# Expert weights that share memory with the rows of x, and quarters in place of whole matrices between the gathers

## The chip, the cores and the metric

The kernel runs on one core of a Trainium2 chip. The metric is device time in microseconds, the median of several executions. Before the change it is 227.68 us (three executions, 227.32 to 227.93). A profiled execution of the same kernel took 224.94 us.

## The reference

Two operations in a row. First a retention recurrence over 4 batches, 8 heads, 768 steps and head size 64; its result becomes 3072 rows x of 512 columns. Then a layer of 8 experts with an early exit: a row with a skip score above 0 goes to the expert with its largest gate logit, and that expert's result is weighted and added to the row; every other row stays as it is.

```
state = gamma * state + k[t] outer v[t];  y[t] = scale * (q[t] @ state)
x = y, heads side by side: 3072 x 512
for rows with x @ w_skip > 0:  e = argmax(x @ w_gate);  g = softmax(x @ w_gate)[e]
    x += g * (relu(x @ w1[e]) @ w2[e])      # w1: 512 x 1024, w2: 1024 x 512
```

## The kernel before, in words

The first stage works on 16 pairs of heads (`for i in range(NU)`), four to a batch. For each pair it turns scaled q and k (`rows_t`), forms chunk states (`kv_states`), scores and values, and multiplies the result by the identity and the gate's columns (`rows_x`, L337), which gives 128 columns of `xall[b]`, the 768 rows of a batch (12 KB in each partition, two buffers in turn), and the gate logits. `store_x` (L355) writes a batch's rows to `out`: for the last batch three stores of 512 KB on SP's queue (L687), for the others on ACT's. Steps of the gate (`gate_a` and on) find for each expert the places of its rows. They come in slots of 128 rows: slot 0 of an expert holds the first 128, slot 1 the next.

The second stage runs over 11 tasks: slot 0 of experts 0, 1 and 2 (k = 0 to 2), slot 1 of the same three (k = 3 to 5), and both slots of experts 3 to 7 (k = 6 to 10). A task casts the gathered rows to bf16 (`cast_rows`, L654), turns them on PE (`turn`, L666), runs `layer1` (L703) and `layer2` (L719), and `scatter` (L519) writes the result rows back. In PE's order the turn of the next task stands between layer 1 and layer 2 of this one. `gather` (L507) and `scatter` are indirect DMAs that POOL issues.

The weights lie in DRAM as f32 and are loaded as bf16, by DMAs that POOL issues too, on the same queue. One expert's w1 or w2 is four quarters (`load_piece`, L199, 256 KB each in bf16) or one whole matrix (`load_whole`, L213, 1 MB). The whole one lies with other rows to a partition, which `inner1` and `inner2` tell to `turn` and `layer1`. All 64 quarters stand in one list, in the order of experts, and whatever comes next is taken from its head. The orders are written out by hand: in the first stage `EARLY` says how many quarters a pair issues and `PLACES` at which of five places in the pair; before each, a small multiplication on POOL (`pool_after`, L538) waits for a result of that place. In the second stage `plan` (L758) gives for each task the steps that follow its layer 2: `Q` a quarter, `W` a whole matrix, `g3.1` the gather of expert 3's slot 1, `s` the scatters of all results so far.

Between the stages POOL issues the gathers of experts 1 and 2 (slot 0), then a drain (L689), a `pool_after` on the last rows, and the steps of `plan[None]`. By then 32 quarters have been issued, the weights of experts 0 to 3.

Of the kernel before, what the change touches and what calls it, by code (L numbers as in the profile page):

```python
# [9 lines left out]
FP32 = mybir.dt.float32  # L10
BF16 = mybir.dt.bfloat16
# [7 lines left out]
def kernel(  # L19
# [18 lines left out]
    PE, V_, A_, G_ = nc.tensor, nc.vector, nc.scalar, nc.gpsimd  # L38

    B, H, S, D = q.shape  # L40
    N, DM = out.shape
    E = moe_w1.shape[0]
    F = moe_w1.shape[2]
    R = 2
    NCH = S // 128
# [8 lines left out]
    NDB = DM // 128  # L54
    NFB = F // 128
# [9 lines left out]
    poolC = ctx.enter_context(tc.tile_pool(name="constp", bufs=1))  # L65
    poolG = ctx.enter_context(tc.tile_pool(name="gpool", bufs=1))
    poolW = ctx.enter_context(tc.tile_pool(name="wpool", bufs=1))

    stM = ExitStack()
    stM.enter_context(tc.manual_schedule())  # L70
# [2 lines left out]
    pool = st1.enter_context(tc.tile_pool(name="rsb", bufs=2))  # L73
# [120 lines left out]

    w1b, w2b, inner1, inner2 = {}, {}, {}, {}

    def load_piece(e, which, c, pl):  # L199
        if which == 0:  # L200
            if not c:
                w1b[e] = pl.tile([128, NDB, F], BF16, tag=f"w1_{e}", bufs=1, name="w1b")
                inner1[e] = 1
            G_.dma_start(out=w1b[e][:, c, :], in_=moe_w1[e][c * 128 : (c + 1) * 128, :])
        else:
            if not c:
                w2b[e] = pl.tile([128, NFB, DM], BF16, tag=f"w2_{e}", bufs=1, name="w2b")
                inner2[e] = NFB // 4
            cs = slice(c * NFB // 4, (c + 1) * NFB // 4)
            rows = moe_w2[e][c * F // 4 : (c + 1) * F // 4, :]  # L210
            G_.dma_start(out=w2b[e][:, cs, :], in_=rows.rearrange("(p a) d -> p a d", p=128))

    def load_whole(n, pl):  # L213
        for _ in range(n):
            if pieces:
                e, which, c = pieces[0]
                assert c == 0
                del pieces[:4]
                t = pl.tile([128, NDB * F], BF16, tag=f"w{which + 1}_{e}", bufs=1, name=("w1b", "w2b")[which])
                cols = (F, DM)[which]  # L220
                (w1b, w2b)[which][e] = t[:, :].rearrange("p (a f) -> p a f", f=cols)
                (inner1, inner2)[which][e] = (NDB, NFB)[which]
                src = (moe_w1, moe_w2)[which][e].rearrange("(p a) f -> p (a f)", p=128)
                G_.dma_start(out=t[:, :], in_=src)

    pieces = [(n // 8, n // 4 % 2, n % 4) for n in range(E * 8)]

    def load_pieces(n, pl):
        for _ in range(min(n, len(pieces))):
            load_piece(*pieces.pop(0), pl)  # L230

# [3 lines left out]
    QKT, St, ATm, Y, xT, xall, Lp = {}, {}, {}, {}, {}, {}, {}  # L235
# [4 lines left out]
    def tps(name="tps"):  # L240
        return psum.tile([128, 512], FP32, tag="T", bufs=2, name=name)
# [95 lines left out]
    def rows_x(i, a):  # L337

        if not 0 <= i < NU:
            return  # L340
        b, p = divmod(i, NP)
        if p == 0 and a == 0:
            xall[b] = pool.tile([128, NCH, DM], FP32, tag="xall", bufs=2, name="xall")
            Lp[b] = pool.tile([128, NP, NCH, NL], FP32, tag="Lp", bufs=2, name="Lp")
        ps = tps()
        for j in range((NCH // 2)):
            PE.matmul(  # L347
                out=ps[:, j * XW : (j + 1) * XW], lhsT=xT[i][:, a * (NCH // 2) + j, :], rhs=IW[:, p, :], start=True, stop=True,
                skip_group_check=True,
            )  # L350
# [149 lines left out]
    def free(ins, others):  # L500
        for o in others:
            tc.declare_no_dep(ins, o.ins, reason="the slots of a pass name distinct rows, empty ones none")

    def rows_of(st, first):
        return (out[0:NOLD, :], NOLD) if first and st == 0 else (out[:, :], N)

    def gather(e, st, first=True):  # L507
        t = xrows[len(gathers) % NROW if first else st]
        src, n = rows_of(st, first)
        ga = G_.indirect_dma_start(  # L510
            out=t[:, :], out_offset=None, in_=src,
            in_offset=bass.IndirectOffsetOnAxis(ap=slot[st][0][:, e : e + 1], axis=0), bounds_check=n - 1, oob_is_err=False,
        )
        xg[e, st] = t
        if first:
            free(ga.ins, scatters)
            gathers.append(ga)
# [13 lines left out]

    EARLY = {0: 1, 1: 1, 2: 1, 3: 2, 4: 1, 5: 1, 6: 2, 7: 2, 8: 1, 9: 1, 10: 2, 11: 3, 12: 4, 13: 5, 14: 4, 15: 1}
    PLACES = {1: (3,), 2: (0, 3), 3: (0, 2, 4), 4: (0, 1, 3, 4), 5: (0, 1, 2, 3, 4)}
    junk = poolC.tile([1, 1], FP32, name="junk")

    def pool_after(x, y=None):  # L538

        G_.tensor_tensor(junk[:, :], x, x if y is None else y, ALU.mult)  # L540

    def weights(i, place, after):

        if place in PLACES.get(EARLY.get(i, 0), ()):
            pool_after(after)
            load_pieces(1, poolW)
# [107 lines left out]
    def cast_rows(e, sts, cast, pl, bufs):  # L654
        xb = []
        for st in sts:
            t = pl.tile([128, DM], BF16, tag="xb", bufs=bufs, name="xb")
            cast(out=t[:, :], in_=xg[e, st][:, :])
            xb.append(t)
        return xb  # L660

    def blocks(rows, a):

        return rows.rearrange("p (c t a) -> p c a t", t=128, a=a)
# [14 lines left out]
    values(NU - 1)  # L679
    b = B - 1  # L680
    pool_after(xT[NU - 1][0:1, 0, 0:1])
    gather(2, 0)
    xb0 = cast_rows(0, [0], V_.tensor_copy, poolG, 1)
    rows_x(NU - 1, 0)
    xgT = turn(0, xb0, V_.tensor_copy, poolG, 1, lambda: psum.tile([128, NDB, 128], BF16, tag="AT0", bufs=1, name="xtp"))
# [10 lines left out]
    poolE = ctx.enter_context(tc.tile_pool(name="esb", bufs=2, reuse_waits="tile"))  # L696
    poolX = ctx.enter_context(tc.tile_pool(name="wlate", bufs=1, reuse_waits="tile"))
# [5 lines left out]
    def layer1(e, xgT):  # L703
        n = xgT.shape[2]
        hT = poolE.tile([128, NFB, CAP], BF16, tag="hT", bufs=2, name="hT")
        m = 512 // n
        for f2 in range(NFB // m):
            ps = psE.tile([128, m, n], FP32, tag="hps", bufs=2, name="hps")
            for f in range(m):
                fb = m * f2 + f  # L710
                for db in range(NDB):
                    PE.matmul(  # L712
                        out=ps[:, f, :], lhsT=blocks(w1b[e][:, db, :], inner2[e])[:, fb // inner2[e], fb % inner2[e], :],
                        rhs=xgT[:, db, :], start=(db == 0), stop=(db == NDB - 1),
                    )
            A_.activation(out=hT[:, m * f2 : m * f2 + m, 0:n], in_=ps[:, :, :], func=AF.Relu, bias=0.0, scale=1.0)  # L716
        return hT

    def layer2(e, sts, hT, first=True):  # L719
        yos = []  # L720
        for k, st in enumerate(sts):
            ps = psE.tile([128, DM], FP32, tag="yps", bufs=2, name="yps2")
            for fb in range(NFB):
                PE.matmul(  # L724
                    out=ps[:, :], lhsT=hT[:, fb, k * 128 : (k + 1) * 128], rhs=w2b[e][:, fb, :],
                    start=(fb == 0), stop=(fb == NFB - 1),
                )
            yo = poolE.tile([128, DM], FP32, tag="yo", bufs=8, name="yo")
            V_.scalar_tensor_tensor(  # L729
                out=yo[:, :], in0=ps[:, :], scalar=slot[st][1][:, e : e + 1], in1=xg[e, st][:, :], op0=ALU.mult, op1=ALU.add  # L730
            )
            if first:
                yos.append((e, st, yo))
            else:
                scatter(e, st, yo, first)
        return yos

    def passes():
# [17 lines left out]
    tasks += [(e, list(range(NST))) for e in range(FIRST, E)]  # L756

    plan = {  # L758
        None: "Q Q", 0: "s", 1: "g0.1 Q g1.1 Q g2.1 W g3.0 s W g3.1", 2: "s g4.0 W g4.1", 3: "s g5.0 W g5.1",
        4: "s g6.0 W g6.1", 5: "s g7.0 W g7.1", 6: "s W",  # L760
    }
    yos = []

    def give(k):
        for step in plan.get(k, "s").split():
            if step == "W":
                load_whole(1, poolX)
            elif step == "Q":
                load_pieces(1, poolX)
            elif step[0] == "g":  # L770
                gather(*(int(n) for n in step[1:].split(".")))
            else:
                while yos:
                    scatter(*yos.pop(0))
# [9 lines left out]
    for k, (e, sts) in enumerate(tasks):  # L784
        hT = layer1(e, xgT)
# [77 lines left out]
```

## Time and profile before

| | us |
|---|---|
| median of three executions | 227.68 |
| profiled execution | 224.94 |
| its span, first to last instruction | 223.2 |
| PE busy | 192.9 (86%) |
| POOL busy | 119.4 (54%) |
| DVE busy | 109.9 (49%) |
| ACT busy | 87.5 (39%) |
| POOL's DMA queue, share of 16 engines | 49.7% |
| mean granted clock of TensorE | 0.971 |

The span in 40 slices of 5.58 us:

```profile
PE   0899998999899997999999888789880799999960
DMA  6979999999999899798799993698999999996211
```

A digit is the busy share of a slice in tenths; the lines count from the span's start. The first stage fills the span up to about 143 us and the second the rest. All times below are from the span's start.

### The profile page before, as it was taken

What the parts mean: (1) busy time and instruction counts of PE and PEld (TensorE: products, weight loads), DVE (VectorE), ACT (ScalarE), POOL (GpSimd) and SP (SyncE); (2) the same over time, 40 slices, a digit from 0 to 9 for tenths busy, and PEclk for the clock granted to TensorE, in tenths of its full rate; (3) what the DMA queues carried; (4) which work ended last, traced back from release to release, by engine and by line L of the source; (5) the groups of instructions that cost most, each with busy time, mean ns of one, the idle gap of its engine ahead of it and who ended that gap; (6) DMA issues with size and microseconds to landing.
All of it is one profiled execution on the core that took longest, in us unless ns stands there. A gap on an engine that the chain in (4) does not pass through costs nothing.

```text
span 223.2 us, 8246 instructions
## 1 busy us (share of the span) xinstructions
PE 192.9 (86%) x3493; PEld 157.1 (70%) x3502; DVE 109.9 (49%) x351; ACT 87.5 (39%) x197; POOL 119.4 (54%) x185
## 2 busy tenths in 40 slices
PE   0899998999899997999999888789880799999960
PEld 0777887897798886798888777765760377678720
DVE  5444535535655566566576786384420253433220
ACT  5324544745435454436455332464240042134210
POOL 2345975765566645746887223428855556523330
PEclk9999999999999999999999999999996599999997
DMA  6979999999999899798799993698999999996211
GB/s 176 247 203 247 280 298 289 236 282 313 245 214 206 222 280 353 179 224 195 117 221 302 215 184 74 145 321 174 181 220 244 246 255 256 267 255 186 90 48 43
DMA packets 49241, 48.73 MB, mean 218 GB/s; under 512 B 3780, under 2 KB 40644, under 8 KB 48304
## 3 DMA queue, kind: packets, MB, share of 16 engines
q0 software_dynamic: 8752, 22.97, 49.7%
q1 hardware_dynamic: 39152, 20.47, 31.7%
q10 hardware_dynamic: 1296, 4.72, 5.6%
q8 instruction: 29, 0.48, 0.8%
q14 instruction: 12, 0.10, 0.1%
HBM read 56.64 MB, written 10.49 MB: 301 GB/s over the span
## 4 chain that ended last, share of the span: by engine, by line
PE 65%; issue 12%; DMA 7%; DVE 6%; POOL 4%; ACT 2%; POOLq 1%; SPq 0%; ACTq 0%; DVEq 0%
PE tps L252 12%; PE tps L347 11%; PE atps L301 10%; PE yps L325 10%; DMA xrows<-out_dram,si 6%; PE kvps L264 6%; PE yps L724 5%; PE yps L281 5%; PE hps L712 4%; POOL out_dram L521 3%; DVE ATm L307 2%; DMA kw<-in_k_dram 1%; POOL xrows L510 1%; PE xtp L673 1%; ACT xT L335 1%
## 5 line engine op out<-in xcount | busy, mean ns | idle before, releaser
L307 DVE TENSOR_TENSOR ATm<-atps,maskc 128x384 f32<-128x384 f32 x64 | 32.9, 553 | 29.6 <-PE atps L301 28.9
L253 ACT COPY QKT<-tps 128x512 f32<-128x512 f32 x48 | 28.1, 587 | 39.7 <-PE tps L252 39.0
L301 PE MATMUL atps<-QKT 64*64 64x128 f32 x768 | 35.4, 271 | 2.0 <-issue 0.9
L716 ACT ACTIVATE hT<-hps 128x512 bf16<-128x512 f32 x32 | 19.0, 597 | 46.0 <-PE hps L712 46.0
L347 PE MATMUL tps<-IW,xT 128*128 128x137 f32 x192 | 29.2, 288 | 2.5 <-ACT xT L335 1.7
L712 PEld LDWEIGHTS <-w1b 128*128 128x128 bf16 x352 | 29.0, 115 | 3.4 <-issue 1.0
L712 PE MATMUL hps<-xgT,w1b 128*128 128x128 bf16 (+1 forms) x352 | 30.7, 246 | 0.6 <-DVE xgT L674 0.6
L724 PE MATMUL yps<-w2b,hT 128*128 128x512 bf16 x119 | 30.5, 396 | 0.5
L301 PEld LDWEIGHTS atps<-QKT 64*64 64x64 f32 x768 | 27.8, 133 | 2.6 <-DVE ATm L307 1.3
L104 POOL TENSOR_TENSOR ks<-kw,tk 128x768 f32<-128x768 f32 x15 | 22.4, 1490 | 12.0 <-DMA kw<-in_k_dram 11.7
L347 PEld LDWEIGHTS tps<-IW,xT 128*128 128x128 f32 x192 | 24.5, 190 | 5.1 <-ACT xT L335 3.4
L325 PE MATMUL yps<-ATm,vn 64*64 64x128 f32 x768 | 26.6, 272 | 1.5 <-issue 1.3
L521 POOL DMA_INDIRECT out_dram<-yo,si x16 | 16.5, 1032 | 20.0 <-DVE yo L729 16.0
L335 ACT COPY xT<-yps 64x384 f32<-64x384 f32 x32 | 15.2, 474 | 25.9 <-PE yps L325 23.5
L252 PE MATMUL tps<-ident,ks 128*128 128x128 f32 x96 | 18.3, 300 | 6.8 <-DVE ks L104 5.3
L325 PEld LDWEIGHTS yps<-ATm,vn 64*64 64x64 f32 x768 | 22.0, 133 | 2.6 <-issue 1.7
L510 POOL DMA_INDIRECT xrows<-out_dram,si x16 | 16.9, 1056 | 12.8 <-DVE g L492 5.6
L104 POOL TENSOR_TENSOR qs<-qw,tq 128x768 f32<-128x768 f32 x15 | 22.4, 1493 | 2.5 <-DMA qw<-in_q_dram 1.3
L729 DVE SCALAR_TENSOR_TENSOR yo<-yps,g,xrows 128x512 f32<-128x512 f32 x16 | 12.0, 750 | 22.9 <-PE yps L724 19.9
L724 PEld LDWEIGHTS <-hT 128*128 128x128 bf16 x128 | 12.3, 101 | 13.6 <-issue 1.7
L281 PE MATMUL yps<-QKT,St 64*64 64x128 f32 x320 | 20.2, 279 | 0.0
L352 ACT COPY xall<-tps 128x384 f32<-128x384 f32 x32 | 15.3, 479 | 10.9 <-PE tps L347 9.0
(113 smaller groups left out, 225.3 us busy)
## 6 DMA issues: line engine op xcount, KB each, us to landing
vn<-in_v_dram SPq DMA_DIRECT2D x16, 384.0 KB, 6.3
kw<-in_k_dram SPq DMA_DIRECT2D x15, 384.0 KB, 5.9
qw<-in_q_dram SPq DMA_DIRECT2D x15, 384.0 KB, 5.2
w1b<-in_moe_w_dram POOLq DMA_DIRECT2D x20, 256.0 KB, 6.1
out_dram<-xall ACTq DMA_DIRECT2D x9, 512.0 KB, 6.9
w2b<-in_moe_w_dram POOLq DMA_DIRECT2D x16, 256.0 KB, 5.3
w2b<-in_moe_w_dram POOLq DMA_DIRECT2D x4, 1024.0 KB, 12.7
w1b<-in_moe_w_dram POOLq DMA_DIRECT2D x3, 1024.0 KB, 12.7
```

The source lines that it names most:

```text
L104: eng.tensor_tensor(o[:, :, h, :], rows[:, :, h, :], sc[:, :, h, :], ALU.mult)
L252: PE.transpose(out=ps[:, j * 128 : (j + 1) * 128], in_=(ks, qs)[w][i][:, s_, :, :].rearrange("p h d -> p (h d)"), identity=ident[:, :])
L253: A_.copy(out=QKT[i][:, 4 * m : 4 * m + 4, :], in_=ps[:, :].rearrange("p (j t) -> p j t", j=4))
L281: PE.matmul(out=Y[i, c][o : o + 64, g, :], lhsT=St[i][t : t + 64, ch - 1, :], rhs=QKT[i][t : t + 64, NCH + R * g : NCH + R * g + R, 64 * c ...
L301: PE.matmul(out=ps[h][cp, j, :], lhsT=QKT[i][hp, a * SPB + j, cp], rhs=QKT[i][hp, NCH + R * g : NCH + R * g + R, cp], start=True, stop=True,)
L307: V_.tensor_tensor(out=ATm[i, a][:, t, :, :], in0=ps[t][:, :, :], in1=maskc[:, a * SPB : (a + 1) * SPB, :, :].rearrange("p s r t -> p s (r ...
L325: PE.matmul(out=Y[i, c][o : o + 64, g, :], lhsT=vn[i][cp, h * G + g, r * D : (r + 1) * D], rhs=ATm[i, a][cp, h, j, :], start=False, stop=l ...
L347: PE.matmul(out=ps[:, j * XW : (j + 1) * XW], lhsT=xT[i][:, a * (NCH // 2) + j, :], rhs=IW[:, p, :], start=True, stop=True, skip_group_che ...
L510: ga = G_.indirect_dma_start(out=t[:, :], out_offset=None, in_=src, in_offset=bass.IndirectOffsetOnAxis(ap=slot[st][0][:, e : e + 1], axis ...
L521: sc = G_.indirect_dma_start(out=dst, out_offset=bass.IndirectOffsetOnAxis(ap=slot[st][0][:, e : e + 1], axis=0), in_=yo[:, :], in_offset= ...
L712: PE.matmul(out=ps[:, f, :], lhsT=blocks(w1b[e][:, db, :], inner2[e])[:, fb // inner2[e], fb % inner2[e], :], rhs=xgT[:, db, :], start=(db ...
L724: PE.matmul(out=ps[:, :], lhsT=hT[:, fb, k * 128 : (k + 1) * 128], rhs=w2b[e][:, fb, :], start=(fb == 0), stop=(fb == NFB - 1),)
```

## The change

A new pool, `rowsp`, holds the two buffers of `xall`; they had been in a pool of the first stage that was given up between the stages. A function `home` now says where each quarter lies. Quarters 0 to 31 and those from 44 on have a tile for four, as before. Quarters 32 to 37 share one buffer of `xall`, quarters 38 and 39 have a small tile, and quarters 40 to 43 share the other buffer of `xall`. The weights are kept as lists of rows, so that a matrix can lie in two places.

The order changes with it. Pair 13 issues four quarters for five, pair 15 four for one. One quarter is issued ahead of the gather of expert 2 and one behind it, before the drain. After task 0 two quarters are issued behind the scatter. After task 1 a quarter stands between gathers where two of the steps were whole matrices; after tasks 2 and 3 two quarters stand for one whole matrix. Whole matrices are loaded for experts 6 and 7 alone, after tasks 4 to 7. The result tile `yo` has seven buffers for eight.

```diff
+    QS = NDB * F // 4
+    NEARLY, NKEEP = 32, 12 * 1024 // (2 * QS)
+    homes, pieces = {}, [(n // 8, n // 4 % 2, n % 4) for n in range(E * 8)]
+
+    def home(n, pl):
+        if n < NEARLY or n >= NEARLY + 2 * 4 + 4:
+            tag, size, first = f"w{n // 4 % 2 + 1}_{n // 8}", 4, n // 4 * 4
+        elif n < NEARLY + NKEEP:
+            tag, size, first = "xall", NKEEP, NEARLY
+        elif n < NEARLY + 8:
+            tag, size, first = "wrest", NEARLY + 8 - (NEARLY + NKEEP), NEARLY + NKEEP
         else:
+            tag, size, first = "xall", NKEEP, NEARLY + 8
+        if first not in homes:
+            bufs = 2 if tag == "xall" else 1
+            homes[first] = (poolP if tag == "xall" else pl).tile([128, size, QS], BF16, tag=tag, bufs=bufs, name="wb")
+        return homes[first][:, n - first, :]
+
+    def load_pieces(k, pl):
+        for e, which, c in pieces[:k]:
+            t = home(e * 8 + which * 4 + c, pl)
+            rows = (moe_w1, moe_w2)[which][e]
+            n = rows.shape[0] // 4
+            part = rows[c * n : (c + 1) * n, :]
+            G_.dma_start(out=t, in_=part.rearrange("(p a) f -> p (a f)", p=128))
+            (inner1, inner2)[which][e] = a = n // 128
...
-            xall[b] = pool.tile([128, NCH, DM], FP32, tag="xall", bufs=2, name="xall")
+            xall[b] = poolP.tile([128, NCH, DM], FP32, tag="xall", bufs=2, name="xall")
...
-    EARLY = {0: 1, 1: 1, 2: 1, 3: 2, 4: 1, 5: 1, 6: 2, 7: 2, 8: 1, 9: 1, 10: 2, 11: 3, 12: 4, 13: 5, 14: 4, 15: 1}
+    EARLY = {0: 1, 1: 1, 2: 1, 3: 2, 4: 1, 5: 1, 6: 2, 7: 2, 8: 1, 9: 1, 10: 2, 11: 3, 12: 4, 13: 4, 14: 4, 15: 4}
...
     pool_after(xT[NU - 1][0:1, 0, 0:1])
+    load_pieces(1, poolW)
     gather(2, 0)
+    load_pieces(1, poolW)
...
-            yo = poolE.tile([128, DM], FP32, tag="yo", bufs=8, name="yo")
+            yo = poolE.tile([128, DM], FP32, tag="yo", bufs=7, name="yo")
...
-        None: "Q Q", 0: "s", 1: "g0.1 Q g1.1 Q g2.1 W g3.0 s W g3.1", 2: "s g4.0 W g4.1", 3: "s g5.0 W g5.1",
-        4: "s g6.0 W g6.1", 5: "s g7.0 W g7.1", 6: "s W",
+        None: "Q Q", 0: "s Q Q", 1: "g0.1 Q g1.1 Q g2.1 Q g3.0 s Q g3.1", 2: "s g4.0 Q g4.1 Q", 3: "s g5.0 Q g5.1 Q",
+        4: "s g6.0 W g6.1", 5: "s g7.0 W g7.1", 6: "s W", 7: "s W",
```

## Rows read from the trace of the kernel before

**Rows 1.** Windows: busy us (instructions) of each engine, granted clock, DMA share, GB/s.

```profile
136.00:138.00 2.00, 1.92 (x48) 1.65 (x48) 1.38 (x10) 0.03 (x1) 1.09 (x1) 1.00 0.00 0
...
146.00:148.00 2.00, 1.79 (x14) 0.95 (x15) 1.86 (x12) 1.38 (x3) 0.30 (x2) 1.00 1.03 414
...
175.00:180.00 5.00, 5.00 (x20) 2.35 (x19) 1.51 (x3) 0.00 (x0) 3.10 (x3) 0.54 1.01 258
```

**Rows 2.** Chain of waits: start, length, what.

```profile
161.11 12.88 DMA xrows<-out_dram,si
```

**Rows 3.** Timeline of PE: start, us, line, operation, count [idle before <- releaser].

```profile
149.84 0.39 PE L673 MATMUL xtp<-identb,xb 128*128 128x128 bf16 x4
...
153.90 1.90 PE L724 MATMUL yps<-w2b,hT 128*128 128x512 bf16 x8
155.98 0.40 PE L673 MATMUL xtp<-identb,xb 128*128 128x128 bf16 x4 [0.19 <-ACT xb L658]
...
164.44 1.95 PE L712 MATMUL hps<-xgT,w1b 128*128 128x128 bf16 x32
...
174.50 0.61 PE L673 MATMUL xtp<-identb,xb 128*128 128x128 bf16 x4 [5.30 <-DVE xb L658]
174.90 3.62 PE L724 MATMUL yps<-w2b,hT 128*128 128x512 bf16 x8
...
178.38 4.27 PE L712 MATMUL hps<-xgT,w1b 128*128 128x256 bf16 x32
...
186.39 3.69 PE L712 MATMUL hps<-xgT,w1b 128*128 128x256 bf16 x32
...
212.20 3.62 PE L724 MATMUL yps<-w2b,hT 128*128 128x512 bf16 x15
```

**Rows 4.** Timeline of ACT, the cast of expert 0's slot 1.

```profile
155.31 0.62 ACT L658 CAST xb<-xrows 128x512 bf16<-128x512 f32 x1 [0.64 <-DMA xrows<-out_dram,si]
```

**Rows 5.** Timeline of POOL between the stages: gather, junk, quarters, scatter, gather, quarter.

```profile
141.93 1.03 POOL L510 DMA_INDIRECT xrows<-out_dram,si  x1 [0.50 <-issue]
147.39 0.18 POOL L540 TENSOR_TENSOR junk<-xall 1x1 f32<-1x1 f32 x1 [4.42 <-ACT xb L658]
147.89 1.14 POOL L204 DMA_DIRECT2D w1b<-in_moe_w_dram  x2 [0.32 <-issue]
150.63 1.06 POOL L521 DMA_INDIRECT out_dram<-yo,si  x1 [1.60 <-DVE yo L729]
151.99 1.06 POOL L510 DMA_INDIRECT xrows<-out_dram,si  x1 [0.30 <-DVE Rsum L424]
153.06 0.59 POOL L204 DMA_DIRECT2D w1b<-in_moe_w_dram  x1
```

**Rows 6.** Lines 689 and 819, the drains: duration ns min/median/max, first and last start.

```profile
L689 POOLq DRAIN  x1: 5516/5516/5516, 141.7 to 141.7; - x1
...
L819 POOLq DRAIN  x1: 4387/4387/4387, 209.7 to 209.7; - x1
```

**Rows 7.** DMA issues, the two at 141.93 and 209.90: us from issue to landing last.

```profile
xrows<-out_dram,si POOLq DMA_INDIRECT x1, 3.8
...
out_dram<-yo,si POOLq DMA_INDIRECT x1, 2.5
```

**Rows 8.** DMA issues of weights, at 119.18, 125.11, 129.43, 186.47 and 192.67 in order.

```profile
w1b<-in_moe_w_dram POOLq DMA_DIRECT2D x1, 256.0 KB, 9.2
...
w1b<-in_moe_w_dram POOLq DMA_DIRECT2D x1, 256.0 KB, 7.0
...
w2b<-in_moe_w_dram POOLq DMA_DIRECT2D x1, 256.0 KB, 5.2
...
w1b<-in_moe_w_dram POOLq DMA_DIRECT2D x1, 1024.0 KB, 12.7
...
w2b<-in_moe_w_dram POOLq DMA_DIRECT2D x1, 1024.0 KB, 13.2
```

**Rows 9.** DMA issue of the gather at 151.99 (expert 0, slot 1).

```profile
xrows<-out_dram,si POOLq DMA_INDIRECT x1, 3.3
```

More of the change, by code (lines that the diff above doesn't have):

```diff
@@ L67 @@
     poolW = ctx.enter_context(tc.tile_pool(name="wpool", bufs=1))
+    poolP = ctx.enter_context(tc.tile_pool(name="rowsp", bufs=1))
     stM = ExitStack()
@@ L197 @@
     w1b, w2b, inner1, inner2 = {}, {}, {}, {}
[L199 to L204, printed above, removed]
-        else:
[L206 to L230, printed above, removed]
+    QS = NDB * F // 4
[8 more added lines that the diff above has]
+            tag, size, first = "wrest", NEARLY + 8 - (NEARLY + NKEEP), NEARLY + NKEEP
+        else:
+            tag, size, first = "xall", NKEEP, NEARLY + 8
[3 more added lines that the diff above has]
+        return homes[first][:, n - first, :]
@@ new lines, in load_pieces @@
+    def load_pieces(k, pl):
[6 more added lines that the diff above has]
+            (inner1, inner2)[which][e] = a = n // 128
+            got = t.rearrange("p (a f) -> p a f", a=a)
+            (w1b, w2b)[which].setdefault(e, []).extend(got[:, j, :] for j in range(a))
+        del pieces[:k]
@@ new lines, in load_whole @@
+    def load_whole(pl):
+        e, which, c = pieces[0]
+        assert c == 0
+        del pieces[:4]
+        rows = (moe_w1, moe_w2)[which][e]
+        (inner1, inner2)[which][e] = a = rows.shape[0] // 128
+        t = pl.tile([128, 4 * QS], BF16, tag=f"w{which + 1}_{e}", bufs=1, name="wb")
+        G_.dma_start(out=t[:, :], in_=rows.rearrange("(p a) f -> p (a f)", p=128))
+        got = t[:, :].rearrange("p (a f) -> p a f", a=a)
+        (w1b, w2b)[which][e] = [got[:, j, :] for j in range(a)]
@@ L712, in layer1 @@
                     PE.matmul(
-                        out=ps[:, f, :], lhsT=blocks(w1b[e][:, db, :], inner2[e])[:, fb // inner2[e], fb % inner2[e], :],
+                        out=ps[:, f, :], lhsT=blocks(w1b[e][db], inner2[e])[:, fb // inner2[e], fb % inner2[e], :],
                         rhs=xgT[:, db, :], start=(db == 0), stop=(db == NDB - 1),
@@ L724, in layer2 @@
                 PE.matmul(
-                    out=ps[:, :], lhsT=hT[:, fb, k * 128 : (k + 1) * 128], rhs=w2b[e][:, fb, :],
+                    out=ps[:, :], lhsT=hT[:, fb, k * 128 : (k + 1) * 128], rhs=w2b[e][fb],
                     start=(fb == 0), stop=(fb == NFB - 1),
                 )
-            yo = poolE.tile([128, DM], FP32, tag="yo", bufs=8, name="yo")
+            yo = poolE.tile([128, DM], FP32, tag="yo", bufs=7, name="yo")
             V_.scalar_tensor_tensor(
@@ L766, in give @@
             if step == "W":
-                load_whole(1, poolX)
+                load_whole(poolX)
             elif step == "Q":
```

## The prediction

> **What bounds the kernel now.** I read the 40 slices of the page first: DMA is full from slice 28 to 36, and PE has one hole there, slice 31. The windows show what follows the hole: from 175 to 180 us PE is busy all the time, at a granted clock of 0.54 [rows 1]. The chain of waits names its cause: from 161.11 us it is one DMA for 12.88 us, the second gather of expert 3 [rows 2]. The PE timeline gives the size [rows 3]. Layer 1 of task 5 (expert 2, second half) ends at 164.44 + 1.95 = 166.39. Next in PE's order stand the transposes of expert 3, and the last four run only at 174.50, because the gather was issued on the queue behind two whole matrices. Then the half clock: eight matmuls of layer 2 take 3.62 us, against 1.90 in task 2, and layer 1 of expert 3 takes 4.27 against 3.69 for expert 4 (0.58). From 166.39 to 178.38 are 12.0 us; with the 0.58 it is 12.6. Unhindered it would be two groups of transposes and eight matmuls, 0.8 + 1.9, some 2.5 us by their overlap. So the hole costs 10.1 us, and after it PE runs without a gap to the last layer 2 at 212.20: what is won there is won at the end, until something else is late.
>
> Two places have no slack. Task 3 (expert 0, second half) transposes at 155.98, right when the cast on ACT ends, and that cast waited for its gather [rows 3, 4]. And POOL, which issues gathers, scatters and weights in one order, stands in a drain from 141.7 for 5.5 us [rows 5, 6].
>
> **The change part by part.**
>
> *Homes and buffers.* Memory only; no instruction is added but twelve quarter issues for three whole ones. The home of quarters 32 to 37 is free once the third batch's rows are stored, which pair 13 begins and pair 15 finds done; the other one waits for the last stores, with k = 1 as its first use. One yo buffer less: the eighth result waits for the first scatter, some 20 us older. I take 0 for these.
>
> *Four more quarters before the second stage* (pair 13 one less, pair 15 three more, two around the gather of expert 2). A quarter takes 1.25 us of the queue: the ones issued at 125.11 and 129.43 land at 132.1 and 134.6, with one between [rows 8]. The extra 5.0 us go where DMA is partly idle: from 136 to 138 its share is 0.00 [rows 1]. But the last of them meet the stores of the last rows, which fill DMA from 146 to 148 (1.03) [rows 1]. The gather of expert 2 now has a quarter ahead of it and the stores beside it; I put its landing at 147.8 instead of 141.93 + 3.8 = 145.7 [rows 5, 7]. PE wants it at 149.84, after a cast of 0.62 [rows 3, 4]: 1.4 us of cover are left, and past them each us costs one.
>
> *The drain.* It names no semaphore. Both drains of the trace outlast the issue before them, and both end a like time after that issue has landed: the first at 147.2, 1.5 us after 145.7; the second at 209.7 + 4.4 = 214.1, 1.7 us after 209.90 + 2.5 = 212.4 [rows 5 to 7]. Counted from the end of the issue they differ more, 4.3 and 3.2. So I read it as waiting for the landing of the last POOL DMA. That is now a quarter, issued about 144.7 (junk, quarter, gather and quarter in a row, by the durations of rows 5). No row shows a drain behind a quarter, so the bounds: if only the issue counts, it ends at 145.3 + 3.2 to 4.3, about 149; if the quarter lands as slowly as the ones beside earlier stores, 9.2 us [rows 8], at 155.4. Between them: some 6.5 us of quarters, gather and stores are left at 144.5, shared between two queues, so the quarter lands at about 150.5 and the drain ends at 152.0. I take that one, 4.8 us later than now.
>
> *Four quarters and a scatter ahead of the first second-half gather.* Behind the drain come junk (0.66 to the next issue), two quarters (1.14), the scatter (0.30 + 1.06), two more quarters (1.16) and 0.30 [rows 5]. The gather is issued at 152.0 + 4.6 = 156.6, against 151.99. It lands 3.3 us later at best, as now [rows 9]. The path from that landing over ACT to PE is the one without slack: task 3 begins 4.6 us later.
>
> *The clock.* PE is then idle from 153.90 + 1.90 = 155.80 to 160.6. The hole of before lowered the clock; I count it lowered once here too, at its price of before: 1.72 in layer 2, 0.58 in layer 1 and some 0.1 in the transposes, 2.4 us. Not lowered it is 0, and I count 2.4 because the nearest row is a hole of the same kind.
>
> *Quarters between the gathers of k = 1.* Now 9.12 us pass from the issue of the first gather to that of expert 3's second. The same steps follow, so it is issued at 165.7, with quarters of 1.25 us ahead of it in place of two whole matrices. It lands some 4.5 us later (3.3 and a quarter's 1.25), at 170.2. PE asks for it at 166.39 + 4.6 + 2.4 = 173.4. The old hole is gone whole: 10.1 us off the path.
>
> *Whole matrices for the last two experts alone.* The last one moves from k = 6 to k = 7. POOL issues 16 gathers or scatters (1.33 us with their gap) and seven weights (0.9) between 165.7 and it, so it is issued at about 194.6 (now 192.67) and lands 13.2 us later at the present load, 207.8 [rows 8]. Layer 2 of the last expert, at 212.20 now, would want it at 212.2 - 3.1 = 209.1. That is cover of 1.3 us, where now it is 6.3.
>
> *By a rule of the skill.* A whole matrix issued at 186.47 and the next at 192.67 land 6.7 us apart with two gathers' and scatters' worth between; four quarters take 5.0 [rows 8]. The Trainium skill, "DMA: Bandwidth & Descriptors", section Bandwidth, says that transfers should be batched to 1 MiB or more for three quarters of the peak, and its section on the anatomy of one DMA puts a fixed part of about 2.0 us on each. By that fixed part, queued, nine further transfers would cost 18 us; by the rows, which overlap it, nothing. The trace disagrees with the queued reading.
>
> **Sum.** Off the path: 10.1. On it: 4.6 (task 3) + 2.4 (clock) = 7.0. Net 3.1 off the span of 223.2, and with what lies around it (224.94 - 223.2 = 1.74, unchanged) 221.8 for the profiled execution. The median of the runs is 227.68, 2.7 above that execution; I take the 3.1, with a little for transposes that no longer run at half clock (0.2), off the median: 224.4.
>
> **Rivals.**
> 1. *The drain waits for the issue only.* For it: a quarter is another kind of DMA than the two indirect ones that were seen; against it the 1.5 and 1.7. Drain to 149, gather at 153.6, landing behind the quarters at about 157, task 3 1.7 late, no fall of the clock: 10.1 - 1.7 = 8.4 off, held to about 8 by the last matrix (POOL 3 us earlier, landing at 204.8, wanted at 203.8). 219.6.
> 2. *The hole only moves.* The quarter lands 9.2 us after its issue, the drain ends at 155.4, task 3 is 8.0 late and the clock falls: 10.4 against 10.1. 227.8, no change.
> 3. *POOL's order becomes the bound: slower.* Everything behind the drain shifts with it, the last matrix too. It lands at 207.8 plus the shift past 152.0, and before it was wanted at 212.2. From 4.4 us of shift, that is a landing of the quarter later than 10.2 us after its issue, the end is later than now, one for one. For it: the stores fill DMA just then. Against it: no quarter of the trace takes 10 us. With 6 us of shift: 229.3.
> 4. *Quarters hold the queue longer than wholes.* At twice 1.25 us the eight quarters from k = 1 on add 10 us and the last matrix comes at 217.8, 5.6 late: 233.3. The landings 2.5 us apart with one between speak against it [rows 8]. The rule above would bring this about.
>
> **How the numbers follow.** Forecast 0.52, its own range 222.5 to 226; rival 1 0.27; rival 2 0.09; rival 3 0.10; rival 4 0.02. Faster by over 0.3% (about what a measurement of this kernel tells from no change): 0.79. Within: 0.09. Slower: 0.12. The range goes from 218.8, under rival 1, to 227.9, over rival 2; it leaves out rivals 3 and 4 and little else.
>
> **What would show it.** The drain's row: an end near 152 or near 149 decides between forecast and rival 1. The cast on ACT for task 3 should begin near 160, and PE show its hole before task 3 and none before expert 3, the low clock about 160 to 168. Expert 3's second gather should land some 4 to 5 us after its issue, not 12.9. The last matrix should land before its layer 2 asks. The forecast is wrong if a hole remains before expert 3, if the gather of expert 2 holds up task 2, or if PE waits for weights at the end.

## The result, and the profile after

The changed kernel took 228.22 us, the median of 20 executions, against 227.67 of 20 of the kernel before. The ratio is 1.010, with a 95% interval of 1.006 to 1.014; it leaves out on both sides the executions over 1.5% above their kernel's fastest, so it isn't the quotient of the two medians, and six of the profiles below (without the first drain, plan alone, control, last behind, task 0's away, best version again) are of such executions. The control below, the kernel before timed against itself, came out at 1.006, so a loss of 1% is near what no change can give. What is clear is that the forecast gain, 224.4 us or 0.986, isn't there. The profiled execution took 229.06 us, its span 227.3.

The 40 slices of the page, after (PE, granted clock, DMA):

```profile
PE   0899998998699999899999878779139999999960
...
PEclk9999999999999999999999999999857999999997
DMA  6879999899998999898799997993999999999501
```

PE has still one empty stretch, in slice 28 (about 160 to 165 us), and the low clock right behind it. Before, the hole was in slice 31. The windows of after over that stretch, in the columns of [rows 1]:

```profile
160.00:165.00 5.00, 0.00 (x0) 0.00 (x0) 0.55 (x1) 0.00 (x0) 4.38 (x7) 0.81 1.09 219
165.00:170.00 5.00, 1.32 (x12) 1.16 (x13) 0.76 (x2) 0.62 (x1) 4.09 (x6) 0.50 1.07 222
```

From 160 to 165 us PE does nothing at all while DMA's share is 1.09; from 165 to 170 the granted clock is 0.50, which is the lower of TensorE's two levels, 1.2 GHz. PE's timeline, after, with the lines that answer to [rows 3]:

```profile
146.50 1.95 PE L724 MATMUL hps<-xgT,wb 128*128 128x128 bf16 x32
149.66 0.40 PE L683 MATMUL xtp<-identb,xb 128*128 128x128 bf16 x4 [1.20 <-ACT xb L668]
...
157.86 1.90 PE L736 MATMUL yps<-wb,hT 128*128 128x512 bf16 x8
168.11 0.61 PE L683 MATMUL xtp<-identb,xb 128*128 128x128 bf16 x4 [8.35 <-ACT xb L668]
169.29 3.57 PE L724 MATMUL hps<-xgT,wb 128*128 128x128 bf16 x32 [0.57 <-DVE xgT L684]
...
178.70 1.95 PE L724 MATMUL hps<-xgT,wb 128*128 128x128 bf16 x32
...
182.69 3.69 PE L724 MATMUL hps<-xgT,wb 128*128 128x256 bf16 x32
...
215.91 3.62 PE L736 MATMUL yps<-wb,hT 128*128 128x512 bf16 x15
```

146.50 is layer 1 of task 0, 169.29 that of task 3, 178.70 of task 5, 182.69 of expert 3. From the start of task 5 to that of expert 3 pass 4.0 us now, against 13.9 before [rows 3]: the old hole is gone. A new one of 8.35 us stands before task 3's transposes, which wait for the cast on ACT:

```profile
148.98 0.62 ACT L668 CAST xb<-xrows 128x512 bf16<-128x512 f32 x1 [1.72 <-DMA xrows<-out_dram,si]
...
167.44 0.62 ACT L668 CAST xb<-xrows 128x512 bf16<-128x512 f32 x1 [8.80 <-DMA xrows<-out_dram,si]
```

Both casts waited for a gather (before: [rows 4]). POOL's timeline, after, says where that gather was, answering to [rows 5]:

```profile
145.83 1.06 POOL L520 DMA_INDIRECT xrows<-out_dram,si  x1 [0.30 <-issue]
146.88 0.59 POOL L225 DMA_DIRECT2D wb<-in_moe_w_dram  x1
157.29 0.18 POOL L550 TENSOR_TENSOR junk<-xall 1x1 f32<-1x1 f32 x1 [9.82 <-issue]
157.72 1.09 POOL L225 DMA_DIRECT2D wb<-in_moe_w_dram  x2 [0.25 <-issue]
159.12 1.05 POOL L531 DMA_INDIRECT out_dram<-yo,si  x1 [0.30 <-issue]
160.18 1.10 POOL L225 DMA_DIRECT2D wb<-in_moe_w_dram  x2
161.58 1.06 POOL L520 DMA_INDIRECT xrows<-out_dram,si  x1 [0.31 <-issue]
```

The last quarter goes out at 146.88, then POOL does nothing for 9.82 us. The drain is line 701 in this kernel; its row, answering to [rows 6], and the landings, in us from the issue, of a store on SP and the quarter at 146.88, of the gather at 161.58 and of expert 3's second gather, issued at 170.67 [rows 2, 7, 9]:

```profile
L701 POOLq DRAIN  x1: 11352/11352/11352, 145.8 to 145.8; - x1
```

```profile
out_dram<-xall SPq DMA_DIRECT2D x1, 512.0 KB, 8.5
wb<-in_moe_w_dram POOLq DMA_DIRECT2D x1, 256.0 KB, 8.6
...
xrows<-out_dram,si POOLq DMA_INDIRECT x1, 5.8
...
xrows<-out_dram,si POOLq DMA_INDIRECT x1, 5.0
```

The quarter lands at 146.88 + 8.6 = 155.5, and the drain ends 1.7 us behind it, at 145.8 + 11.35 = 157.15 (157.12 before rounding). The gather that task 3 needs is issued at 161.58 and lands 5.8 us later.

**Where the time went.** Executions of one program differ in the length of the first stage: layer 1 of task 0 starts at 143.32 in the profile of before and at 149.76 in another execution of it (the control below). So I count from that start, T0. "Task 3" and the rest are the starts of their layers 1, from PE's timelines; "end" is the span less T0. Two kernels were profiled twice, and their starts of task 3 agree within 0.15 us when counted so.

| us from T0 | before | before, control | after |
|---|---|---|---|
| first drain ends | 3.9 | 2.1 | 10.6 |
| task 3 | 13.65 | 13.80 | 22.79 |
| task 5 | 21.12 | 22.08 | 32.20 |
| expert 3 | 35.06 | 34.56 | 36.19 |
| expert 7 | 65.35 | 64.28 | 65.89 |
| end | 79.9 | 78.6 | 80.8 |

Task 3 comes 9.1 us later, half clock makes it 11.1 at task 5, and the old hole gives 9.95 back. What is left is 0.5 to 1.6 us at expert 7 and 0.9 to 2.2 at the end. The measured 1% is 2.3 us: against the control the second stage accounts for it, against the first profile for less than half. How much of it lies in the first stage, whose spread of 6 us hides it, stays open.

### The profile page after: what moved, and what is told of

It is laid out like the page before. It is cut to its first block, busy times and chain, and to the rows that moved or that the text cites. A ratio compares the mean times of both kernels' runs of the same rounds, so it can differ in the third digit from the quotient of the medians.

```text
span 227.3 us, 8260 instructions
## 1 busy us (share of the span) xinstructions
PE 192.7 (85%) x3493; PEld 157.8 (69%) x3502; DVE 109.2 (48%) x351; ACT 87.5 (39%) x197; POOL 125.3 (55%) x196
## 5 line engine op out<-in xcount | busy, mean ns | idle before, releaser
L311 PE MATMUL atps<-QKT 64*64 64x128 f32 x768 | 35.9, 272 | 3.4 <-issue 2.4
L724 PE MATMUL hps<-xgT,wb 128*128 128x128 bf16 (+1 forms) x352 | 31.8, 251 | 0.6 <-DVE xgT L684 0.6
L724 PEld LDWEIGHTS <-wb 128*128 128x128 bf16 x352 | 29.3, 111 | 3.8 <-issue 0.7
L225 POOL DMA_DIRECT2D wb<-in_moe_w_dram x48 | 27.7, 577 | 6.2 <-issue 5.0
L736 PE MATMUL yps<-wb,hT 128*128 128x512 bf16 x119 | 28.8, 379 | 0.7 <-issue 0.2
L345 ACT COPY xT<-yps 64x384 f32<-64x384 f32 x32 | 15.1, 473 | 27.6 <-PE yps L335 25.1
```

The lines of the kernel that those rows point to most:

```text
L225: G_.dma_start(out=t, in_=part.rearrange("(p a) f -> p (a f)", p=128))
L311: PE.matmul(out=ps[h][cp, j, :], lhsT=QKT[i][hp, a * SPB + j, cp], rhs=QKT[i][hp, NCH + R * g : NCH + R * g + R, cp], start=True, stop=True,)
L724: PE.matmul(out=ps[:, f, :], lhsT=blocks(w1b[e][db], inner2[e])[:, fb // inner2[e], fb % inner2[e], :], rhs=xgT[:, db, :], start=(db == 0) ...
L736: PE.matmul(out=ps[:, :], lhsT=hT[:, fb, k * 128 : (k + 1) * 128], rhs=w2b[e][fb], start=(fb == 0), stop=(fb == NFB - 1),)
```

## The experiments

All kernels but the control and the last two are the changed kernel with an edit. They were timed in three groups (four, four and two kernels), each beside executions of the kernel before on the same chip; ratios are to these. Times "behind T0" are counted as in the table.

**Without the first drain.**

```diff
-    G_.drain()
```

> The changed kernel without the drain between the stages, nothing else. Theory (the drain waits for the landing of the last quarter, 11.4 us in the changed kernel, and all behind it on POOL is late): the gather of expert 0's slot 1 is issued within 8 us of the start of the second stage's first layer 1 (15.1 in the changed kernel, 8.7 before), the hole of 8.4 us ahead of task 3 shrinks below 2 us, the hole ahead of expert 3 stays away, no low clock; span 8 to 9 us under the changed kernel's at a like start of the second stage, ratio to before 0.96 to 0.97. Rival (the four quarters and the scatter ahead of that gather in the queue make it late, whatever the drain does): a hole of 4 us or more stays ahead of task 3, ratio 0.985 to 1.0.

Measured: 0.999 of the kernel before (0.993 to 1.005), so 1% better than the changed kernel. POOL's timeline shows what comes in the drain's place, PE's the hole that remains:

```profile
158.95 1.06 POOL L520 DMA_INDIRECT xrows<-out_dram,si  x1 [2.73 <-DMA out_dram<-xall]
...
163.50 0.40 PE L683 MATMUL xtp<-identb,xb 128*128 128x128 bf16 x4 [3.80 <-ACT xb L668]
```

Now the gather waits for the stores, the rows that it reads from. It goes out 12.5 us behind T0 instead of 15.1, and the cast on ACT that waits for it begins 3.9 us after that issue instead of 5.9: task 3 at 18.03 instead of 22.79, against 13.65 before. So the drain is about half of the delay, where the theory took it for all (gather within 8 us, hole under 2). The other half is there without it: the stores took 8.8 us (before: 4.6). In this profile nearly all that is won, 4.2 us at expert 7, is lost at the end (80.7 behind T0, 80.8 after), where the other drain stands 9.0 us, 5.5 after and 4.4 before [rows 6]; the 1% by which the times are better doesn't show in it.

**Both quarters around the gather of expert 2 behind the drain.**

```diff
-    load_pieces(1, poolW)
     gather(2, 0)
-    load_pieces(1, poolW)
...
-        None: "Q Q",
+        None: "Q Q Q Q",
```

> The changed kernel with the drain kept, and the two quarters that stood around the gather of expert 2 moved behind the drain (four quarters there in place of two). Theory: the last landing ahead of the drain is the gather's again, so the drain ends some 1.6 us after it, 5 to 6 us after it begins; the gather of expert 0's slot 1 then has six quarters ahead of it in the queue (7.5 us) and lands some 2.5 us later than before, hole of 2 to 3 us ahead of task 3, no low clock, ratio 0.965 to 0.975. Rival (quarters ahead in the queue are the cost): no better than the changed kernel, 1.0 to 1.01.

Measured: 0.990 (0.986 to 0.994), faster than the kernel before. The drain, and PE before task 3:

```profile
L699 POOLq DRAIN  x1: 6601/6601/6601, 144.0 to 144.0; - x1
...
164.35 0.61 PE L683 MATMUL xtp<-identb,xb 128*128 128x128 bf16 x4 [6.29 <-ACT xb L668]
```

The drain ends 5.0 us behind T0 (10.6 after), as the theory had it. Yet task 3 comes only 2.9 us sooner, at 19.94, with a hole of 6.29 us for the theory's 2 to 3, and still at low clock (its layer 1 takes 3.57 us for 1.95): six quarters now stand behind the drain ahead of the gather of expert 0. The quarters have a price on either side of the drain.

**The plan of quarters alone, the early quarters as before.**

```diff
-        ... 13: 4, 14: 4, 15: 4}
+        ... 13: 5, 14: 4, 15: 1}
...
-    load_pieces(1, poolW)
     gather(2, 0)
-    load_pieces(1, poolW)
...
-        None: "Q Q", 0: "s Q Q",
+        None: "Q Q", 0: "s",
...
-        4: "s g6.0 W g6.1", 5: "s g7.0 W g7.1", 6: "s W", 7: "s W",
+        4: "s g6.0 Q g6.1 Q", 5: "s g7.0 W g7.1 W", 6: "s W", 7: "s W W",
```

> The order between the gathers alone: as many early quarters as before the change (32, none around the gather of expert 2), two behind the drain, none behind task 0's scatter, quarters between the gathers up to task 4, whole matrices for the rest, two after task 5 and two after task 7. Theory: drain and task 3 as before the change; the second gather of expert 3 has quarters ahead of it and lands 4 to 6 us after its issue, no hole ahead of expert 3; ratio 0.955 to 0.965 if the weights keep up. Rival (the lead of six quarters is what pays for the rest): PE waits for weights of experts 5 to 7, holes of 2 us or more there, ratio 0.975 to 1.0.

Measured: 1.015 (1.009 to 1.021), slower. Neither hole is there, task 3 at 13.96 and expert 3 at 27.63 behind T0, 7.4 us sooner than before. All of it and more is given back at the end, where PE waits for weights, as the rival had it (the theory's ratio was 0.955 to 0.965):

```profile
201.49 5.38 PE L722 MATMUL hps<-xgT,wb 128*128 128x256 bf16 x32 [3.12 <-DMA wb<-in_moe_w_dram]
...
213.71 3.75 PE L722 MATMUL hps<-xgT,wb 128*128 128x256 bf16 x32 [2.47 <-DMA wb<-in_moe_w_dram]
```

So the quarters between the gathers cure the old hole, as the change meant, and task 3 is as early as before without the early quarters. But four quarters fewer ahead of the second stage are 1 MB more in it, and they come slower in this form. The same stretch of three kernels, in the columns of [rows 1], the kernel before with whole matrices, after and this one with quarters between gathers and scatters:

```profile
175.00:185.00 10.00, 9.95 (x59) 5.98 (x59) 3.53 (x12) 2.39 (x4) 6.77 (x7) 0.77 1.03 244
```

```profile
175.00:185.00 10.00, 9.95 (x114) 7.85 (x114) 5.72 (x16) 3.35 (x6) 8.19 (x9) 1.00 0.94 203
```

```profile
175.00:185.00 10.00, 10.00 (x82) 7.43 (x80) 5.19 (x14) 3.63 (x7) 8.46 (x10) 1.00 0.91 201
```

With quarters DMA moves 201 to 203 GB/s and is not quite full (0.91 to 0.94), with whole matrices 244 at 1.03. The stretches hold gathers and scatters too, so this isn't the rate of the weights alone.

**The kernel before once more, as a control.**

> The kernel before, once more. In the two profiles the second stage's first layer 1 starts at 143.3 us before the change and at 146.5 after it. If that is a spread of executions: this profile starts it anywhere between 143 and 147, and the ratio is 1.0 within 0.4%. If the change lengthens the first stage: 143 to 144 again here, and 146 or more in each experiment that keeps the early quarters.

Measured: 1.006 (1.002 to 1.011) against the other executions of itself. The same program differs from itself by more than the 0.3% that the prediction took for the measurement's bound, and by more than half of the changed kernel's 1.0%. Its T0 is 149.76, outside both of the ranges above, so one profile each doesn't tell whether the change lengthens the first stage. Its other numbers are the second column above; the hole before expert 3 is there again (1.25 and 5.01 us in its two transposes).

**Only the last quarter behind the drain.**

```diff
     gather(2, 0)
-    load_pieces(1, poolW)
...
-        None: "Q Q",
+        None: "Q Q Q",
```

> The changed kernel with one thing moved: the second of its two quarters at the gather of expert 2 is issued behind the drain of POOL instead of ahead of it; the first stays ahead of that gather. Theory (the drain waits until the last transfer that POOL issued has landed, and that quarter took 8.6 us beside the stores where the gather ahead of it takes some 4 to 5): the drain ends some 1.6 us after the landing of the gather of expert 2, so 5 to 6 us earlier than in the changed kernel's profile against the start of task 0 (10.6 us behind it there); one more quarter then stands ahead of the next gather, so task 3 comes some 4 us earlier; time 0.987 to 0.995 of the kernel before, as with both quarters behind the drain (0.990). Rival (the bytes beside the stores delay the drain, not which transfer is last): the drain ends as late as in the changed kernel, and the time is 1.005 to 1.015 of the kernel before.

Measured: 0.992 (0.984 to 1.000), in the theory's range, but not by its way. The gather of expert 2, issued at 143.42, and the drain:

```profile
xrows<-out_dram,si POOLq DMA_INDIRECT x1, 8.3
...
L700 POOLq DRAIN  x1: 10372/10372/10372, 142.9 to 142.9; - x1
```

The gather, now the last transfer ahead of the drain, itself takes 8.3 us behind one quarter and beside the stores (their median 7.5 us), where the theory took 4 to 5; in the changed kernel it already took 6.4. The drain ends 9.2 us behind T0, 1.4 us sooner than after and not 5 to 6. So the theory that the last quarter's own landing makes the delay fell: one quarter ahead of the gather is enough to make gather and stores late. The gather lands at 143.42 + 8.3 = 151.7. DMA in the two microseconds up to then, in the columns of [rows 1]:

```profile
150.00:151.00 1.00, 1.00 (x7) 0.49 (x6) 0.99 (x6) 0.07 (x1) 0.00 (x0) 1.00 0.44 176
151.00:152.00 1.00, 1.00 (x21) 1.00 (x19) 0.87 (x5) 0.29 (x1) 0.00 (x0) 1.00 0.20 66
```

Its share is down to 0.44 and 0.20 there, so it isn't a full DMA that holds the gather at the last; what does, no run shows.

**The two quarters of task 0 behind the gathers.**

```diff
-        0: "s Q Q", 1: "g0.1 Q g1.1 Q g2.1 Q g3.0 s Q g3.1",
+        0: "s", 1: "g0.1 Q g1.1 Q g2.1 Q g3.0 s Q g3.1 Q Q",
```

> The changed kernel with one thing moved: the two quarters that it issues behind the results of task 0, ahead of the gather of expert 0, go behind the second gather of expert 3; the drain is as in the changed kernel. Theory (two causes add up: the drain, and POOL's order behind it, each quarter ahead of that gather holding it by its issue and by the transfers in the queue): the drain ends as late as before, the gather of expert 0 is issued some 1.5 to 2 us earlier against the drain's end and lands in 4 to 5 us instead of 5.8, so task 3 comes 2 to 4 us earlier; time 0.993 to 1.003 of the kernel before. Rival (the drain alone is the delay, the quarters behind it lie beside what the gather waits for anyway): no change against the changed kernel, 1.005 to 1.015.

Measured: 0.998 (0.987 to 1.008); the interval takes in both theories, so the trace decides. Landings of a store, of the last quarter ahead of the drain, and of the gather of expert 0:

```profile
out_dram<-xall SPq DMA_DIRECT2D x1, 512.0 KB, 8.1
wb<-in_moe_w_dram POOLq DMA_DIRECT2D x1, 256.0 KB, 9.2
...
xrows<-out_dram,si POOLq DMA_INDIRECT x1, 4.8
```

The drain is as late as after (11.3 us behind T0). The gather lands in 4.8 instead of 5.8 us, and task 3 comes at 21.29, 1.5 us sooner; less than the 2 to 4 expected. At the end PE waits 1.85 us for weights, which come later here, and in this profile the end itself is later than after (83.9 behind T0 against 80.8).

**Two quarters between drain and gather, none ahead of the drain; whole matrices late.**

```diff
-    load_pieces(1, poolW)
     gather(2, 0)
-    load_pieces(1, poolW)
...
-        None: "Q Q", 0: "s Q Q", 1: "g0.1 Q g1.1 Q g2.1 Q g3.0 s Q g3.1", 2: "s g4.0 Q g4.1 Q", 3: "s g5.0 Q g5.1 Q",
-        4: "s g6.0 W g6.1", 5: "s g7.0 W g7.1", 6: "s W", 7: "s W",
+        None: "Q Q", 0: "s", 1: "g0.1 Q g1.1 Q g2.1 Q g3.0 s Q g3.1 Q Q Q Q", 2: "s g4.0 g4.1 W", 3: "s g5.0 g5.1 W",
+        4: "s g6.0 g6.1 W", 5: "s g7.0 g7.1 W", 6: "s W",
```

> The 34 early quarters as in the changed kernel, but none around the gather of expert 2 and none ahead of the gather of expert 0 except the two at the start of the second part; quarters between the gathers of tasks 1, then the rest of expert 5's first matrix behind the second gather of expert 3, and five whole matrices, one behind the gathers of each of tasks 2 to 6. Theory (both the drain and the queue ahead of the gather are taken away, and the weights still come by large transfers late): the drain ends about 1.6 us behind the landing of expert 2's gather, task 3 comes as early as in the kernel before, within 2 us, and expert 3 has no hole; 0.965 to 0.985 of the kernel before. Rival (what the plan of quarters between gathers alone showed: POOL cannot issue weights fast enough between the gathers, so the last experts wait for their weights): stalls of 3 us or more for weights in the last 35 us, 0.99 to 1.015.

Measured: 0.977 (0.972 to 0.982); it beats both kernels and is called the best version below. The first drain; landings of a store and the gather of expert 2 ahead of it, and of the gather of expert 0 behind it; then PE before task 3 and before expert 4, and POOL's last scatters:

```profile
L699 POOLq DRAIN  x1: 6508/6508/6508, 141.8 to 141.8; - x1
```

```profile
out_dram<-xall SPq DMA_DIRECT2D x3, 512.0 KB, 4.8
...
xrows<-out_dram,si POOLq DMA_INDIRECT x1, 4.7
...
xrows<-out_dram,si POOLq DMA_INDIRECT x1, 4.3
```

```profile
157.16 0.40 PE L683 MATMUL xtp<-identb,xb 128*128 128x128 bf16 x4 [0.86 <-ACT xb L668]
...
174.23 0.73 PE L683 MATMUL xtp<-identb,xb 128*128 128x128 bf16 x8 [0.96 <-DVE xb L668]
```

```profile
201.76 0.98 POOL L531 DMA_INDIRECT out_dram<-yo,si  x1 [0.74 <-DVE yo L739]
211.04 0.98 POOL L531 DMA_INDIRECT out_dram<-yo,si  x1 [8.29 <-issue]
212.32 0.98 POOL L531 DMA_INDIRECT out_dram<-yo,si  x1 [0.30 <-issue]
```

With no quarter around the gather the stores land in 4.8 us, near the 4.6 of before, and the drain ends 4.9 us behind T0. Task 3 comes at 14.71, expert 3 at 26.17, 8.9 us sooner than before, with no half clock. Expert 7 is 8.2 us sooner (57.12), the end only 4.6 (75.3): the second drain stands 8.65 us, because the scatter issued at 201.76 lands behind the last whole matrix, and the last scatter goes out at 212.32, though its rows are ready at 209.04.

**All of these early.** As the last one, but with its two quarters in the first stage too.

```diff
-        ... 14: 4, 15: 4}
+        ... 14: 5, 15: 5}
...
-        None: "Q Q", 0: "s",
+        None: "", 0: "s",
```

> As the run with two quarters at the start of the second part, but these two are also issued in the first stage (36 there: five instead of four in pairs 14 and 15), so that nothing at all stands between the drain and the gather of expert 0 except the results of task 0. Theory (the drain and the queue ahead of the gather make the delay): task 3 comes as early as in the kernel before or earlier, expert 3 has no hole; 0.960 to 0.985 of the kernel before, and at least as fast as its sister. Rival (quarters in the last pairs hold POOL and the queue and so the first stage's end, or the gathers of experts 1 and 2, landing late beside them): the second part starts or task 1 waits 1 us or more later than in the sister run, which is then the faster one by 0.5 to 1.5%.

Measured: 0.988 (0.983 to 0.994), slower than its sister by 1.1%. PE before task 1 and before expert 4:

```profile
148.49 0.40 PE L683 MATMUL xtp<-identb,xb 128*128 128x128 bf16 x4 [1.53 <-ACT xb L668]
...
177.33 0.81 PE L683 MATMUL xtp<-identb,xb 128*128 128x128 bf16 x8 [2.42 <-DVE xb L668]
```

Task 3 comes no sooner (14.77). POOL's first scatter shows why:

```profile
152.97 1.02 POOL L531 DMA_INDIRECT out_dram<-yo,si  x1 [2.05 <-DVE yo L739]
```

It stands ahead of the gather of expert 0 and waits for the result of task 0, here for 2.05 us; the sister issues her two quarters in this wait, and 0.62 us of it are left. What the gather gains by having none ahead (it lands in 3.3 us for 4.3), a drain 0.5 us later and a slower way to layer 1 take back. Task 1 waits for its gather (1.53 us against 0.83 in the sister) and expert 4's transposes for theirs (2.42 against 0.96). So the result is nearer the rival, with less than its 1 us at task 1. Of the 1.1%, 2.5 us, the second stage shows 0 to 1.2 at the end, by the sister's two profiles; the rest stays open.

**The second drain one task earlier**, in the best version.

```diff
-        if k == len(tasks) - 2:
+        if k == len(tasks) - 3:
```

> The version with two quarters at the start of the second part (0.977 of the kernel before), with POOL's last drain one task earlier, behind the results of the last but two instead of the last but one. In that version's profile this drain stands from 201.5 to 210.2 and the last two scatters go out at 211.04 and 212.32, though their rows are ready at 207.32 and 209.04. Theory (the drain waits for the landing of the last scatter before it, which is queued behind the last whole matrices): it now ends near 204, holds only the scatters of the last but one task, which nothing waits for, and the last scatter goes out near 209.7, so 2.0 to 2.8 us are saved: 0.963 to 0.970 of the kernel before. Rival (the end waits for all transfers anyway, so later scatters of the last but one task push the last ones by as much): no gain over its sister, 0.974 to 0.980.

Measured: 0.976 (0.970 to 0.983), its sister beside it 0.978: no gain. The drain and the first scatter behind it:

```profile
L829 POOLq DRAIN  x1: 14402/14402/14402, 196.1 to 196.1; - x1
...
211.34 0.98 POOL L531 DMA_INDIRECT out_dram<-yo,si  x1 [12.27 <-DVEq L832]
```

The theory had the drain end near 204, 60.6 us behind its version's T0. Counted from T0 (144.93 here) it starts at 51.2, 7.0 us sooner than in the best version's profile, but ends at 65.6, only 1.2 sooner, since the scatters ahead of it are again behind the whole matrix issued at 190.80. Four scatters, 1.3 us apart, then follow it instead of two, and the last goes out at 70.3, against 68.9. What is queued decides here, not where the drain stands.

**The best version again.**

> The version with two quarters at the start of the second part once more, unchanged, beside the run with the earlier drain. Theory (its gain is that of the program and not of one execution): 0.972 to 0.982 of the kernel before, task 3 starting 13.5 to 15.5 us behind task 0 and task 6 (expert 3) 25.5 to 27.5 us behind it. Rival (the spread from one execution to the next carries its lead): a ratio over 0.985, or task 3 later than 16 us behind task 0.

Measured: 0.978 (0.972 to 0.985). Task 3 at 14.81, expert 3 at 27.72, a little over the 25.5 to 27.5 expected; the end is at 76.6. The gain is that of the program.

## Why the prediction was wrong

*What held.* The old hole went away whole: 9.95 us, and 0.58 of half clock behind it (forecast 10.1). In the control it was 8.5. The clock fell once before task 3, at 1.9 us by task 5 (forecast 2.4). The drain does wait for a landing and not for the issue, so rival 1 is out; over all kernels it ended 1.5 to 1.9 us behind the landing of the last DMA that POOL had issued, save in the one case below. PE waits for no weights at the end after (215.91 is 212.39 + 3.52, as between other layers), so rivals 3 and 4 are out as mechanisms, though the time came near rival 3's. It was close: the last matrix, issued at 200.00, took 15.0 us for the 13.2 of the forecast and landed 0.9 us before its layer 2, although that began 3.6 us later from T0 than forecast. Had PE alone kept to the forecast, it would have waited for this matrix. Expert 3's second gather landed 5.0 us after its issue (forecast some 4.5). Homes, buffers and their waits showed no cost.

*What failed: the shift of task 3, 4.6 us forecast and 9.1 measured.* Counted from T0, three terms carry it.

- The drain's end was put at 152.0 - 143.3 = 8.7 us; it came at 10.6. The step that failed is the landing of the last quarter, put 5.8 us behind its issue by sharing some 6.5 us of work; it took 8.6, near the upper bound of 9.2. That is 2.8 us; as the quarter went out 1.0 us sooner from T0 than forecast, 1.9 of them reach the drain's end.
- Order behind the drain: 4.6 forecast from its end to the gather's issue, 161.58 - 157.15 = 4.4 measured. This one held.
- The gather's landing, "3.3 us later at best, as now", was taken as the value although four quarters had been put ahead of it on its queue. It took 5.8: 2.5 us. The 3.3 was a row of a gather with two quarters ahead, issued some 4 us before it. I had priced the same neighbourhood at 1.25 us a quarter for expert 3's gather, and not here.

The rest, 0.2, lies between landing and layer 1, where the transposes ran at half clock (0.61 us for 0.40). The prediction also gave expert 1's gather no delay; it landed 5.2 us after its issue at 143.74, and PE stood 1.20 us before task 1. That stall is inside the drain's cover, so it costs nothing further.

So rival 2 ("the hole only moves") describes the trace: quarter 8.6 for its 9.2, task 3 9.1 late for its 8.0, no hole before expert 3. Its time, 227.8, was near, in part by luck: it put the whole 8.0 on the drain, where the drain came 6.7 us later and the gather's landing made the 2.5 that this rival didn't price either. I gave it 0.09.

*What the runs put in the place of the failed step.* The price of a quarter depends on what it stands beside and what is behind it:

| kernel | quarters ahead of drain, behind it ahead of gather | stores | drain ends | task 3 | ratio |
|---|---|---|---|---|---|
| before | 0, 2 | 4.6 | 3.9 | 13.65 | 1 |
| plan alone | 0, 2 | 4.8 | 4.0 | 13.96 | 1.015 |
| best version | 0, 2 | 4.8 | 4.9 | 14.71 | 0.977 |
| all early | 0, 0 | 5.5 | 5.4 | 14.77 | 0.988 |
| both behind | 0, 6 | 5.6 | 5.0 | 19.94 | 0.990 |
| last behind | 1, 5 | 7.5 | 9.2 | 22.04 | 0.992 |
| task 0's away | 2, 2 | 8.1 | 11.3 | 21.29 | 0.998 |
| after | 2, 4 | 8.5 | 10.6 | 22.79 | 1.010 |

("Ahead of drain" counts those around the gather of expert 2; "stores" is the median landing of the last three; ends and starts in us from T0.) From the best version, two quarters ahead of the drain add 6.6 us to task 3 (21.29 - 14.71), 3.3 each; the two more at task 0 add 1.5. Together they are the 8.1 that separate after from it. Four more quarters behind the drain, with none ahead of it, add 5.2, 1.3 each and near the 1.25 of the queue that the prediction used elsewhere. The first two there cost nothing against the first stage (14.71 and 14.77): they are issued while POOL would wait for task 0's result. A quarter ahead of the drain costs more than its queue time: with one there the gather took 8.3 us for 4.7 and the stores 7.5 for 4.8, and the drain waits for the last landing of POOL's; without the drain the gather of expert 0 waits for the stores. That these prices hold is shown by the runs; why one quarter of 1.25 us makes the others 3 us later is shown only in part. The Trainium skill, "DMA: Bandwidth & Descriptors", section on queues, rings and completion order, says that a DMA engine takes turns between its queues packet by packet; the stores at 8.1 to 8.5 us with two quarters around the gather and at 4.8 with none agree with that. The batching rule of its section Bandwidth, which the prediction weighed and gave no price, is borne out in its direction: 203 GB/s with quarters against 244 with whole matrices. Its three quarters of the peak, no run here tests.

Why the change gains nothing, then: 10 us of hole are removed, and the quarters put around the drain to make that possible cost 11 us at task 3 and in the half clock behind it. Leaving these out, with whole matrices again from task 2 on (best version), keeps 8.9 us at expert 3 and 4.6 at the end, 7.3 and 3.3 in its second profile.

## What to carry to other kernels

Price a prefetch by the landings of everything that shares its time on the DMA engines and waits behind it, not by its issue or its own queue time: here a quarter cost 0 to 3.3 us by place alone. Where a gather feeds a path without slack, count the transfers ahead of it one by one, and do not take its landing from a row with fewer ahead. When a hole is removed by moving transfers earlier, ask which wait will end on them; the cure here was to move only those that nothing on the path stood behind.

## What was not expected of the hardware

A drain on POOL ends a short time behind the landing of POOL's last DMA, and that time grew with the DMAs that POOL had issued since the drain before:

| DMAs since the drain before | kernel, drain | from landing to end, us |
|---|---|---|
| 35 | before, first | 1.48 |
| 39 | after, first | 1.65 |
| 43 | after, second | 1.80 |
| 45 | both behind, second | 1.88 |
| 82 | without the first drain, its only one | 3.40 |

Between the first and last that is about 0.04 us for each DMA, and all 23 drains in these two places of the twelve profiles lie within 0.01 us of that line. (Landings here are taken from the trace's semaphore events.) The time since the drain before doesn't set it: it is over 140 us for a first drain and 45 to 65 for a second, and both lie on the line. In the kernel without its first drain this is 1.6 of the 3.5 us by which the drain at the end stands longer than after; the rest is a scatter that landed 1.9 us later.

And the first stage of the same program ended 6.4 us apart in the two profiles of the kernel before, and 3.1 in the two of the best version, so a change of that size there can't be read from one profile each.
